# A new engine order, fewer filling matmuls and fewer normalisation shifts in a recurrent attention and gated MLP kernel

## Chip, core and metric

The kernel runs on one core of a Trainium2 chip. The metric is device time in microseconds (us), median over runs. The names of the engines are PE (TensorE), DVE (VectorE), ACT (ScalarE), POOL (GpSimd) and SP (SyncE, which here only issues DMAs).

## What is computed

A gated linear recurrence over 768 steps for 4 batches and 8 heads of width 48, followed by a gMLP block whose spatial mixing runs over the 768 steps:

```python
for t in range(S):                      # B, H, S, D = 4, 8, 768, 48
    state = alpha[:, :, t, :, None] * state + einsum('bhd,bhe->bhde', k[:, :, t], v[:, :, t])
    y[:, :, t] = einsum('bhd,bhde->bhe', q[:, :, t], state)
x = y.transpose(0, 2, 1, 3).reshape(B, S, H * D)
h = maximum(x @ w_in, 0.0)              # 384 -> 1024
u, v = h[..., :512], h[..., 512:]
v_n = (v - mean(v)) / sqrt(var(v) + 1e-06)
v_s = einsum('ts,bsd->btd', w_spatial, v_n) + b_spatial[None, :, None]
out = ((u * v_s) @ w_out)               # 512 -> 384, float32
```

## The kernel before

The recurrence is worked in chunks of 128 steps, six to a batch, 24 in all. Inside a chunk the decays are summed as logarithms by a matmul with a triangle (`cum`, and `half` for the first part of a sum over two), and the exponentials of the sums scale the keys (`kt` = k times the inverse product `binv`) and the queries (`qt`). Matmuls then make transposes of both (`tr`, `trk`), the chunk's contribution to the state (`upd`), masked scores (`sc`; the mask is applied by DVE: `ms`, `m`) and the output (`y`), which also takes the state before it. The state goes on in DVE and POOL: `z` adds the old state, `S` multiplies by the chunk's decay, `sb` copies it to bf16. Chunks 0 to 3 and 6 to 9 are worked four at a time (`four_chunks`), chunks 4 and 5 as a pair, the others two by two; a `j` in a key counts pairs of chunks, an `i` single chunks. The first number of a key in the MLP is the batch.

The MLP has for each batch the projections `v` (with its eviction `ve`) and `u` (`ue`), normalisation (`bn` statistics on DVE, `rs` the reciprocal deviation on ACT, `nm` the shift, `vn` the normalised rows), spatial mixing `s(b, d, th, part)` (the product with the transposed spatial weights: four matmuls, then two), its eviction with bias `se` on DVE, the gate `g` (tile gT) on POOL or DVE, and the output projection `o` with eviction `oe` and store. The weights come in float32 and are cast (`cast`); the spatial weights are transposed by PE (`wt`) and evicted (`we`).

Nothing here is scheduled by the framework. All operations are collected in a list `ops`, and the string `PLAN` gives the order in which they are emitted: a word is an engine's letter (P, D, A, G for POOL, S for SP) and the operation's number, after `@` the PSUM banks that it takes, after `:` filling matmuls ahead of it, written as columns, kind and bank (`512#7`: a float32 matmul of 512 columns on constant data into bank 7). Each engine works its own instructions in the order in which the words stand. Most evictions and products may run on one of two or three engines, and the letter decides which. `replay` reads the plan. Helpers record all matmuls of the projections and of the mixing on line 1006, all PSUM copies on lines 179 and 181, the products with `mul` on line 190, the filling matmuls on line 243, the shifts on line 1085, `vn` on lines 1093 (ACT) and 1097 (DVE).

`vn` has two forms. On ACT it is scale times input plus a shift, and needs the shift −mean/deviation; on DVE it subtracts the mean and multiplies, and does not read the shift:

```python
                if e == "ACT":
                    nc.scalar.activation(
                        out=vn[n2][:, x, :], in_=v_sb[n2][:, x, :], func=AF.Identity, bias=shift[n2][:, x:x + 1],
                        scale=rstd[n2][:, x:x + 1])
                    return
                nc.vector.tensor_scalar(
                    out=vn[n2][:, x, :], in0=v_sb[n2][:, x, :], scalar1=mvs[n2][:, x, 0:1],
                    scalar2=rstd[n2][:, x:x + 1], op0=ALU.subtract, op1=ALU.mult)
```

Of the kernel before, what the change touches and what calls it, by code (L numbers as in the profile page):

```python
# [37 lines left out]
LETTERS = {"P": "PE", "D": "DVE", "A": "ACT", "G": "POOL", "S": "SP"}  # L38
# [1 line left out]


PLAN = """
D2 D0 D4 D1 G9 G11 G5 G6 D3 S56 S57 S59 S58 A60 S12 S169 S170 A61 S272 S171 D8 P62@0:512#0:512#0:512#0 P66@1 P67 P63
P70@2 P71 P74@3 P75 A68 A64 D79 G82 P91@4,5 P52@6 A69 A72 A76 G7 A78 A92 A84 A65 G88 G87 A73 A77 D85 D90 D81 D93 D53
D83 D80 P103@6,4,5,7:512#7:424#7 P94@0,1 D86 D104 D89 D106 G13 P97@6,2:192#2 D98 A95 P100@3,0 D101 A96 P117@3,6:376#1
P115@4,1 A99 G107 G14 A15 A173 D102 D109 P128@0,2 D119 D118 P174@5 A116 A122 A176 P130@6,4 S16 D132 D131 S172 A135
P175@1 A129 P120@3 P54@2 G110 G105 P136@0,4 A121 A178 A55 G111 G108 P133@6 G181 A180 A134 G184 A179 D112 A177 D138
P123@7,3 P141@2 S20 G276 G277 G278 G17 G19 G18 D124 D125 P151@6 P187@7,4 P126@3 S23 S274 S273 D185 A152 A127 G186 G183
G113 G114 D182 P190@5,6 A189 A192 A142 P144@3 D137 P139@4 D188 D191 A140 G22 G21 D153 D143 P199@6,5 P196@2,7 P162@4
A280 A145 P287@0 A163 P154@1 P160@3 A279 A288 A155 D200 D201 D198 D197 D164 P193@4 A161 P156@7 A157 A165 D194 D146  # L50
P158@5 A159 G195 P202@1,2 P203 S26 A204 A147 D166 P290@4 P37@5,7 D38 P34@3,6 G24 S275 S384 S396 G25 S503 S29 D35
P207@1 D148 D208 D36 A39 A289 P205 P281@7 P40@3,5 A206 A282 A167 G10 D42 P210@2 D149 D150 D41 S385 S386 D168 D209 S398
S397 P284@5 P223@6 P219@3 P221@1 A211 A291 A224 A285 D212 A283 A220 A213 D295 D301 A286 A292 D214 D222 D215 A216
P225@6 P233@2 P217@3 P229@7 P237@0 A218 A28 D298 G297 G27 D304 G294 P226 D227 G300 G303 P43@3,5 D45 P230 P234 D231
D235 A293 A44 P46@4,6 P306@5,1 D308 P238 P49@7,3 D50 D51 A48 A47 A307 P309@2,6 P315@1,4 P312@5,7 P249@3 P250 A310 A316
A314 A296 A311 A299 D313 D317 D239 G236 D251 P338@4,1 P332@7,5 P245@0 P246 G302 G305 D333 D339 G232 P318@7,6,3,2 G240
G228 D340 D319 A507 G33 D334 D321 D247 P253@4 P330@7,1 P254 P241@5 P242 G320 A388 A400 A30 A337 A331 A32 G322 P389@0
D255 P345@7,6 D243 D324 D347 A390 P341@4 A391 P335@5 G31 G325 D394 D327 D346 G393 P401@3 A342 A336 A402 A403 P257@1
A392 S492 S387 A258 P259@4 P356@2 S399 G404 G248 G323 G326 S491 S557 P343@0,7 D405 P351@3,5 P407@1,6 A357 D328 A344
A350 A408 D353 D352 P359@2 G252 G395 P348@7 A349 P354@3 D409 S505 S494 S506 P418@6,1 P413@5,0 D358 S493 S504 S559 S547  # L60
S545 S608 S558 S548 S546 A355 A360 D415 D420 P508@7 P366@3 P410@0 P371@2 P377@1 D411 D414 A260 A509 P375@0 D419 A495
D361 A372 A561 P262@5 P496@6 G244 G329 G406 G256 A367 A376 A510 D368 G412 A497 A498 P416@0 P421@3 A422 G514 G502 G500
D378 D379 D513 G512 A417 P264@2 P267@4 A499 A362 A380 A268 D363 D501 P426@0 P423@1 P435@3 P437@6 D381 A365 A427 A424
P433@4 A434 A438 A382 D263 D436 P269@0 D364 D265 D425 D428 D383 P518@1 P369@4 A511 A270 P562@6 P373@2 A374 A429 A549
P439@7 A565 P526@0 D440 D519 P453@3 D430 D431 A432 A563 A564 D370 P449@7 P550@1 P515@2,5 A516 A551 A553 D517 A552 P454
D455 D527 D567 G566 G520 G554 G456 P441@4 P442 P445@5 D443 P450 D451 P465@6 P446 D555 D447 P530@7,4 P521@2,0 P569@1,3
D522 G448 G452 P469@5 P466 P457@2 P470 D523 D531 D532 G528 G444 D471 S620 A556 P572@7 D573 A570 P458 S622 S609 S560
A612 D467 D459 P613@4 P524@5 P533@1 A624 S610 A571 P576@7,3 P585@6,0 G574 A614 A525 D586 A615 A534 P625@5 A626 A568
G472 P535@2 A627 P461@1 S621 S611 S727 S715 S718 S623 S717 G617 D618 D578 D577 S730 S729 P473@6 G628 G575 P538@3
P581@7 A536 A616 A539 P462 S781 S716 A474 D629 P631@5,4 D587 A633 D463 D582 S728 A719 P588@3 S783 S769 S782 S770 S832  # L70
S771 A589 S784 S772 G619 G529 P579@1 A580 D632 D537 P634@7 P479@6 A630 A480 P720@5 G583 G468 D635 G636 A721 P642@3,4
P637@0,2 D540 G460 G584 P476@7 P601@6 P593@1 D643 D639 D638 A731 A723 D644 G726 G464 A602 A738 G724 P590@3 P597@6 A591
P732@0 D603 D592 A735 D477 P645@4 P640@3 A541 D542 D543 D594 A646 P485@2 A641 A785 A598 A486 D544 P650@4 P657@7 P742@6
A651 D743 D652 A733 A604 D605 D607 P488@3 P661@4 A658 A662 A734 P647@6 A489 A773 G736 P595@1 D648 D606 P482@4 D649
A483 A722 D744 P663@7 A664 D737 P599@6 P659@4 P786@3 A653 A600 P673@7 P669@0 P750@6 A596 A787 A788 P774@1 A775 A789
A776 S481 S844 S833 S834 A836 A780 S835 S845 A660 S846 D654 D655 D656 D751 D725 P674 P670 P677@6 P685@5 D671 P678
P665@0 D791 D752 D675 D779 G778 G792 D679 P796@7 P666 G790 D797 P686 G672 D687 D667 P739@6,4 P793@7,3 A848 A777 D794
P693@5 A740 A795 G680 G676 P805@0 P694 P849@7 P837@6 A838 A839 A850 A840 A851 D741 P745@3,4 P754@1,2 D695 G798 G668
D746 D806 D755 P689@5 P690 D691 D747 P681@3 P700@0 P682 P697@5 G843 D756 A698 D683 P703@4 D853 D842 D704 A701 P757@5
A758 P748@0 A749 A799 P800@6,7 D802 G841 G852 P809@3,2 P855@4,5 G807 G684 G696 G688 A856 G692 D810 P759@0 S847 P858@7  # L80
P762@3 D811 D801 P709@2 P812@6 A753 A760 P803@0 A857 D859 D761 D854 A813 A804 A763 P861@5,7 P866@4,1 S699 P712@6 D863
# [51 lines left out]
def kernel(  # L133
# [23 lines left out]
    NDS = DH // 128  # L157
# [70 lines left out]
    vn = sb("vn", 2, [128, NT, DH])  # L228
# [37 lines left out]
    ops, made = [], {}  # L266
# [788 lines left out]
    def project_v(b, tt):  # L1055
# [20 lines left out]
        def rs(_):  # L1076
# [3 lines left out]

        op(("rs", b, tt - 1), "ACT", rs,
           [("bn", b, tt - 1), ("bn", b, tt), ("vn", b - 2, tt - 1), ("vn", b - 2, tt), ("zeros", 3)])
        def nm(_):
            for x in (tt - 1, tt):
                nc.vector.tensor_scalar(
                    out=shift[n2][:, x:x + 1], in0=mvs[n2][:, x, 0:1], scalar1=rstd[n2][:, x:x + 1], scalar2=-1.0,
                    op0=ALU.mult, op1=ALU.mult)
# [188 lines left out]
```

## Time and profile before

| | us |
|---|---|
| median of 3 runs | 138.48 |
| lowest, highest | 137.95, 138.50 |
| profiled execution | 139.19 |
| its span in the trace | 137.4 |
| PE, DVE, ACT, POOL busy | 131.0, 120.8, 108.0, 87.2 |

The span is the time from the first to the last instruction in the trace; what the profiled execution took beyond it lies around it. Lines of the profile name the source line, the engine, the operation, and the tiles as out<-in without buffer numbers. In a timeline the first number is the start, the second the time that the row's instructions cover; a bracket at the end gives idle time ahead of the row and what ended it. In a table of groups stand count, busy time, mean duration in ns, and idle time ahead. The ends of matmuls are modelled, so the distance between starts says more than a matmul's own length.

### The profile page before, as it was taken

To read this page: it belongs to the slowest core of one execution; us is meant where nothing else is said; L and a number is where in the kernel's file an instruction comes from. 1 tells how busy PE (TensorE), PEld (TensorE's weight loads), DVE (VectorE), ACT (ScalarE), POOL (GpSimd) and SP (SyncE) were. 2 spreads that over 40 slices of the span, in tenths; PEclk is the share of its full clock that TensorE was granted. 3 is DMA by queue.
4 is the path that set the end of the run, shared out by engine and by line. 5 is a ranking of instruction groups with operands and counts; after the bars stand their busy time and mean duration, and the time that the engine had idled before them with its cause. 6 is when DMAs were issued, how large, how long until landed. Compare 5 with 4: busy or idle time off the path is not lost.

```text
span 137.4 us, 5308 instructions
## 1 busy us (share of the span) xinstructions
PE 131.0 (95%) x2122; PEld 79.2 (58%) x2122; DVE 120.8 (88%) x300; ACT 108.0 (79%) x261; POOL 87.2 (63%) x146
## 2 busy tenths in 40 slices
PE   6899998999999999999999999999999999999990
PEld 3365554564646566566657666656566765565560
DVE  6259999979999999999899999997999999974871
ACT  3476998899989889999997989999965796954041
POOL 7365899967399789972079989620799842003560
PEclk9999999999999999999999999999999999999999
DMA  3999999599989796899999797899991497101055
GB/s 83 371 371 382 341 321 347 132 374 383 366 164 261 159 218 127 163 184 192 195 190 209 143 205 147 167 194 226 190 181 23 158 390 257 66 0 57 0 203 203
DMA packets 76473, 28.66 MB, mean 209 GB/s; under 512 B 63008, under 2 KB 74912, under 8 KB 76448
## 3 DMA queue, kind: packets, MB, share of 16 engines
q1 hardware_dynamic: 76416, 28.32, 78.6%
q8 instruction: 16, 0.26, 0.8%
q14 instruction: 9, 0.07, 0.2%
q0 software_dynamic: 32, 0.00, 0.0%
HBM read 23.60 MB, written 4.72 MB: 206 GB/s over the span
## 4 chain that ended last, share of the span: by engine, by line
PE 76%; ACT 6%; DVE 6%; DMA 5%; issue 3%; POOL 2%; SPq 0%; POOLq 0%; ACTq 0%
PE bank L1006 53%; DMA kc<-in_k_dram 5%; PE bank L961 3%; PE bank L945 3%; PE bank L989 3%; PE bank L417 2%; PE bank L855 2%; PE bank L899 2%; PE bank L837 2%; PE bank L933 2%; DVE vn L1097 1%; PE bank L795 1%; PE bank L772 1%; ACT uT L185 1%; DVE w_spT L181 1%
## 5 line engine op out<-in xcount | busy, mean ns | idle before, releaser
L1006 PE MATMUL bank<-w_spT,vn 128*128 128x384 bf16 x192 | 35.8, 327 | 0.3 <-DVE vn L1097 0.3
L190 POOL TENSOR_TENSOR gT<-vs,uT 128x384 bf16<-128x384 f32 x28 | 25.7, 933 | 14.3 <-DVE vs L1153 14.1
L190 POOL TENSOR_TENSOR kt<-kc,binv 128x384 bf16<-128x384 f32 x22 | 20.3, 931 | 20.3 <-ACT binv L909 15.2
L1006 PEld LDWEIGHTS <-vn 128*128 128x128 bf16 x192 | 17.4, 98 | 11.7 <-DVE vn L1097 0.7
L1006 PE MATMUL bank<-w_in,xT 128*128 128x512 bf16 x72 | 19.1, 380 | 0.2 <-ACT xT L179 0.2
L1006 PE MATMUL bank<-xT,w_in 128*128 128x384 bf16 x96 | 18.7, 326 | 0.0
L1006 PE MATMUL bank<-w_out_sb,gT 128*128 128x384 bf16 (+1 forms) x100 | 18.4, 320 | 0.0
L1153 DVE TENSOR_TENSOR vs<-bank,bsp_bc 128x384 f32<-128x384 f32 x31 | 16.3, 550 | 2.4 <-PE bank L1006 2.3
L950 DVE TENSOR_TENSOR ptm<-bank,mask 128x512 bf16<-128x512 f32 x28 | 17.9, 683 | 0.4 <-PE bank L945 0.2
L179 ACT COPY kqT<-bank 128x512 bf16<-128x512 bf16 (+1 forms) x20 | 15.0, 792 | 3.1 <-PE bank L989 1.9
L1068 DVE BATCH_NORM_STATS2 stats<-v_sb 128x6 f32<-128x512 bf16 x24 | 16.4, 682 | 0.2
L185 ACT ACTIVATE v_sb<-bank 128x512 bf16<-128x512 f32 x20 | 11.8, 599 | 1.8 <-PE bank L1006 1.5
L185 ACT ACTIVATE uT<-bank 128x384 bf16<-128x384 f32 x27 | 12.4, 495 | 0.7 <-PE bank L1006 0.6
L1006 PEld LDWEIGHTS <-w_in 128*128 128x128 bf16 x96 | 9.0, 98 | 6.7 <-DVE ptm L950 0.3
L190 DVE TENSOR_TENSOR qt<-qc,bank 128x384 bf16<-128x384 f32 x24 | 12.6, 545 | 0.2 <-DMA qc<-in_q_dram 0.2
L1006 PEld LDWEIGHTS <-gT 128*128 128x128 bf16 x100 | 9.3, 98 | 5.8
L179 ACT CAST xT<-bank 128x384 bf16<-128x384 f32 x23 | 10.4, 482 | 1.8 <-PE bank L417 1.4
L844 DVE TENSOR_TENSOR ptm<-bank,mask 128x512 bf16<-128x512 f32 x16 | 10.4, 684 | 0.0
L1006 PEld LDWEIGHTS <-xT 128*128 128x128 bf16 x72 | 6.2, 97 | 6.2 <-ACT xT L179 1.2
L179 ACT COPY raw_w<-bank 128x384 f32<-128x384 f32 x8 | 3.8, 480 | 7.3 <-PE bank L1006 7.2
L394 DVE TENSOR_TENSOR zs<-bank,state 128x384 f32<-128x384 f32 x16 | 8.8, 549 | 0.5 <-PE bank L933 0.4
L243 PE MATMUL bank<-junk 128*128 128x512 f32 (+3 forms) x14 | 8.0, 700 | 1.1 <-DVE junk L1242 1.1
(162 smaller groups left out, 265.4 us busy)
## 6 DMA issues: line engine op xcount, KB each, us to landing
ac<-in_alpha_dram SPq DMA_DIRECT2D x14, 192.0 KB, 4.4
kc<-in_k_dram SPq DMA_DIRECT2D x14, 192.0 KB, 4.0
qc<-in_q_dram SPq DMA_DIRECT2D x14, 192.0 KB, 4.4
vc<-in_v_dram SPq DMA_DIRECT2D x14, 192.0 KB, 4.1
raw_w<-in_moe_w_spatial_dram SPq DMA_DIRECT2D x3, 768.0 KB, 8.0
out_dram<-o_sb SPq DMA_DIRECT2D x9, 192.0 KB, 2.0
ac<-in_alpha_dram SPq DMA_DIRECT2D x2, 768.0 KB, 6.8
kc<-in_k_dram SPq DMA_DIRECT2D x2, 768.0 KB, 7.6
```

The costliest lines, as they stand in the source:

```text
L179: nc.scalar.copy(out=out, in_=in_)
L185: nc.scalar.activation(out=out, in_=in_, func=AF.Relu)
L190: ENG[eng].tensor_tensor(out=out, in0=in0, in1=in1, op=ALU.mult)
L243: nc.tensor.matmul(out=banks[n][:, 0:cols].rearrange("p (a b) -> p a b", a=4), lhsT=junk, rhs=junk[:, None, 0:cols // 4].to_broadcast([128 ...
L394: lambda _: nc.vector.tensor_tensor(out=zs[i % 3], in0=tp(), in1=state[(i - 1) % 3], op=ALU.add),
L844: nc.vector.tensor_tensor(out=ptm[n2][:, ci, s], in0=banks[sl.bank].rearrange("p (hp t) -> p hp t", hp=HP), in1=mask[:, 3][:, None, :].to_ ...
L945: nc.tensor.matmul(out=pt[s][:, hp, :], lhsT=kT[rows, hp, :], rhs=qT[rows, hp, :], start=True, stop=True)
L950: nc.vector.tensor_tensor(out=ptm[n2][:, ci, s], in0=banks[sl_p[s].bank].rearrange("p (hp t) -> p hp t", hp=HP), in1=mask[:, 2][:, None, : ...
L961: nc.tensor.matmul(out=place(to, 3 * hp + (0, 1, 1, 2)[x]), lhsT=heads(vb, hp, x), rhs=ptm[n2][:, ci, x // 2, hp, :], start=(turn == 0), s ...
L1006: nc.tensor.matmul(out=ps, lhsT=lhsT, rhs=rhs, start=first and n == 0, stop=last and n == len(pairs) - 1)
L1068: nc.vector.bn_stats(out=stats[tt % 2], in_=v_sb[n2][:, tt, :])
L1153: nc.vector.tensor_tensor(out=vs[d], in0=banks[sl.bank][:, 0:TH], in1=bsp_bc[:, th, :], op=ALU.add)
```

## The change

Three things are changed.

- `PLAN` is a new string. The order on SP is the same as before; on PE, DVE, ACT and POOL it is another, and so are banks. For a number of operations the engine is another. Over the whole run DVE gets five more key products (`kt`, `kts`: 2 before, 7 after) and four more gates (4, then 8) from POOL, four more `vn` from ACT (18, then 22), and gives three `ve` to ACT (4, then 1) and two `S` to POOL; POOL gives five of its 13 `sb` to ACT or DVE. POOL has 111 operations before and 97 after, ACT 234 and 237.
- The filling matmuls stand at the same places. Ahead of the first sums they have 512, 512 and 512 columns before and 512, 512 and 360 after; ahead of the first state update 512 and 424, then 512 and 160; ahead of the transposes of the second keys 192, then 104; ahead of the first scores 376, then 232.
- The shift `nm` was one operation for two row tiles and always computed both (24 instructions). It is now one operation for each row tile and emits nothing where the `vn` of that tile runs on DVE. `vn` runs on ACT for two tiles after, so two shifts are left. `replay` sets each operation's engine ahead of the replay so that `nm` can see it.

```diff
 PLAN = """
-D2 D0 D4 D1 G9 G11 G5 G6 D3 S56 S57 S59 S58 A60 S12 S169 S170 A61 S272 S171 D8 P62@0:512#0:512#0:512#0 P66@1 P67 P63
-P70@2 P71 P74@3 P75 A68 A64 D79 G82 P91@4,5 P52@6 A69 A72 A76 G7 A78 A92 A84 A65 G88 G87 A73 A77 D85 D90 D81 D93 D53
...
+S56 D0 S57 G6 D1 S59 G10 D2 D3 G5 S58 G9 D8 D4 A60 G11 S12 A61 P62@0:512#0:512#0:360#0 P70@1 P66@2 P63 P67 A64 P71
+S171 A68 P74@3 D79 A72 P75 D82 S172 D85 P91@4,5 A76 P52@6 G87 A93 D88 G90 A53 D92 A84 D81 G7 S275 A77
...
 """
...
 def replay(ops, held, warm, plan):
 
+    for word in plan.split():
+        op = ops[int(re.match("[A-Z]([0-9]+)", word).group(1))]
+        op.eng = LETTERS[word[0]]
     for word in plan.split():
...
-        def nm(_):
-            for x in (tt - 1, tt):
+        for x in (tt - 1, tt):
+            def nm(_, x=x):
+                if made[("vn", b, x)].eng == "DVE":
+                    return
                 nc.vector.tensor_scalar(
                     out=shift[n2][:, x:x + 1], in0=mvs[n2][:, x, 0:1], scalar1=rstd[n2][:, x:x + 1], scalar2=-1.0,
                     op0=ALU.mult, op1=ALU.mult)
 
-        op(("nm", b, tt - 1), "DVE", nm, [("rs", b, tt - 1), ("vn", b - 2, tt - 1), ("vn", b - 2, tt)])
-        for x in (tt - 1, tt):
+            op(("nm", b, x), "DVE", nm, [("rs", b, tt - 1), ("vn", b - 2, x)])
+
             def vnf(e, x=x):
...
             op(("vn", b, x), "DVE ACT", vnf,
-               [("rs", b, tt - 1), ("nm", b, tt - 1)] + [("s", b - 2, d, th, 1) for d in range(NDS) for th in range(2)])
+               [("rs", b, tt - 1), ("nm", b, x)] + [("s", b - 2, d, th, 1) for d in range(NDS) for th in range(2)])
```

More of the change, by code (lines that the diff above doesn't have):

```diff
@@ L48 @@
[L48 to L57, printed above, removed]
@@ new lines @@
+D187 P139@1 A145 D184 G19 A17 D18 G281 P192@4,2 D191 S23 P157@5 A194 D193 S277 A140 D146 P201@2,4 G185 A282 S276
+P198@7,6 P161@1 G188 D202 A153 G114 P159@0 D200 A283 G22 P195@2 D203 P163@6 A162 D196 A147 P155@1 A160 G197 D150 D199
+P287@2 A158 D154 P204@7,0 A164 G21 A288 P207 D165 P205 G24 P37@6,5 A208 S26 P34@4,3 A206 D151 D148 S278 P212@0 G25
+A289 D38 S389 D39 A166 P209@7 A213 D169 D35 D36 P224@4 D167 D149 A210 S401 D214 P293@0 A156 P290@3 A225 P43@7,5 D301
+A168 P40@1,6 P222@4 D45 D170 A41 P226@5 D211 A291 P284@1 A42 P220@2 G303 A294 P236@6 A215 A285 D216 D218 D227 D44 D306
@@ new lines @@
+A374 D386 A446 S555 D518 P524@4 P272@0 A429 D380 A376 P569@3 D367 S553 P431@2 A520 D388 A268 D430 P459@5 A432 P451@1
+A572 D433 S628 A570 P467@2 A571 A434 P455@7 S630 A556 D437 D507 D525 D438 D435 P532@6 P447@4 A273 S617 D436 D533
+P557@0 D573 P452 G534 S567 A558 P441@6 D574 A620 P448 D453 A563 P460 S618 G561 D449 A560 P521@3,1 A559 D461 P468 G454
+S629 A632 D562 P579@5 A442 P456 D580 G450 A523 P463@0 S619 D469 P633@5 D522 P439@6 G462 S736 A634 P464 D457 A440
+P527@3,1 D465 P576@2,4 S724 G458 D529 P536@6,7 A577 P475@0 G526 D537 S727 G581 P621@1 D538 A575 P443@6 S631 A635 D578
@@ new lines @@
+P476 A622 P471@7 D528 A623 G625 P472 A627 D637 P588@3 P485@4 A444 D477 G636 A624 D626 P530@6 S726 A486 P539@0 G466
+D473 A531 P592@4,1 D589 A728 S739 P639@7,5 G474 D594 A540 P583@3,6 A740 P541@2 D593 S738 G478 A641 P642@1 D640 P741@4
+S791 P544@0 G590 A542 D584 A535 P479@7 D470 G591 S725 A742 D585 P482@3 A545 G582 D643 P729@2 S737 G638 A483 P595@0
+D546 A480 G735 P586@3 S793 A596 D543 P650@7,1 A730 P645@0,6 A587 P608@5 D652 A547 P600@3 A743 D647 S779 A732 P494@1
+D651 G733 A795 P597@6 S792 D646 A495 G644 A731 P491@7 D746 A744 S780 D734 D548 D550 G745 P796@0 A598 P602@4 A609 S843
@@ new lines @@
+P648@6 G747 A601 D610 P653@5 P748@3,2 A654 D599 P751@1 A492 S781 P658@5 A603 D752 A649 P604@7 A659 S794 P759@6 P666@1
+A611 A749 P655@5 S782 D614 D612 D753 D549 D750 D660 P670@2 A656 D615 S487 P606@3 D613 A797 D551 P488@5 A667 D657 G800
+S855 A783 P672@4 S844 A798 D671 P678@1 A607 S845 A661 P784@2 P682@3 A847 D664 D801 D662 D489 D665 A785 P674@5 S846
+D663 A787 G788 D760 A786 P683 S856 A799 P675 D789 G761 P686@6 A605 D684 A673 P679 S857 D676 A790 G685 P754@4,3
+P803@7,2 D755 S858 G677 P763@5,0 A804 P687 D680 P668@4 D688 A802 P690@1 D765 G689 A859 P691 D764 P848@0 G681 P694@6
@@ new lines @@
+P718@2 A836 D775 D778 P885@0 D837 A719 P895@7 A838 P882@2 D839 D841 D886 D840 P715@0 A883 D842 P897@3 A776 D884 P893@2
+A830 P909@5 D887 A898 A896 P921@6 D894 A832 A888 P901@7 A722 D889 D891 D892 P905@4 A716 D890 S723 P913@0 S717 P910
+P914 D911 P902 P906 D915 G912 P899@5 D903 P917@0 D907 A900 G904 D916 P918 P922 P929@5 D919 P930 D908 G920 P925@0 D923
+P926 D931 P938@6 D927 P932@5 D928 A939 D924 P935@0 S940 A933 P941@6 S934 D936 S720 P947@5 A942 S937 P944@0 D948 S943
+P950@5 A945 S949 A951 S946 S952
```

54 lines of the change are left out of this document (20 added, 34 removed).

## The prediction

> **What bounds the kernel now.** I read the page first, then busy time by stage, then the order of time on single engines.
>
> ```profile
> span 137.4 us, 5308 instructions
> PE 131.0 (95%) x2122; PEld 79.2 (58%) x2122; DVE 120.8 (88%) x300; ACT 108.0 (79%) x261; POOL 87.2 (63%) x146
> PE 76%; ACT 6%; DVE 6%; DMA 5%; issue 3%; POOL 2%; SPq 0%; POOLq 0%; ACTq 0%
> ```
>
> The chain that ended last is three quarters TensorE (PE), but VectorE (DVE) is busy 88%. By stage (engine busy us in each stretch):
>
> ```profile
> core 0: us, PE busy (x) PEld busy (x) DVE busy (x) ACT busy (x) POOL busy (x), PEclk, DMA share, GB/s
> 8.40:15.40 7.00, 6.76 (x158) 4.06 (x155) 6.79 (x15) 5.55 (x14) 4.90 (x9) 1.00 1.11 366
> 15.40:25.00 9.60, 8.66 (x228) 5.02 (x231) 9.36 (x19) 8.33 (x21) 9.32 (x15) 1.00 1.02 327
> 25.00:38.50 13.50, 13.20 (x212) 7.30 (x202) 12.48 (x34) 13.20 (x33) 9.16 (x17) 1.00 0.97 313
> 38.50:60.00 21.50, 21.46 (x501) 13.46 (x502) 21.00 (x44) 19.74 (x47) 19.05 (x27) 1.00 0.85 179
> 8.40:96.30 87.90, 86.38 (x1604) 52.86 (x1602) 84.11 (x192) 80.49 (x200) 63.22 (x91) 1.00 0.95 235
> 96.30:134.20 37.90, 37.83 (x506) 23.25 (x504) 33.21 (x72) 23.63 (x57) 19.92 (x38) 1.00 0.47 140
> ```
>
> From 38.5 us PE has no gap worth naming. Up to 96.30 DVE is free for only 87.90 − 84.11 = 3.79 us, of which 0.21 + 0.24 + 1.02 fall before 38.5 and 2.32 after, where it mostly waits for a later PE. So two engines are nearly full over 88 us, and PE is the one that sets the end. I therefore cut the run at one block that both versions have: s(2,2,0,1), the second part of batch 2's first mixing product, which needs the last normalised rows vn of batch 2 from DVE.
>
> ```profile
> 8.40 1.55 DVE L190 TENSOR_TENSOR kt<-kc,binv 128x384 bf16<-128x384 f32 x2 [3.59 <-ACT binv L741]
> 95.16 0.73 DVE L1097 TENSOR_SCALAR vn<-v_sb,mvs,rstd 128x512 bf16<-128x512 bf16 x2
> 96.32 1.14 PE L1006 MATMUL bank<-w_spT,vn 128*128 128x384 bf16 x6
> 134.22 0.36 DVE L181 COPY raw_w<-bank 128x192 f32<-128x192 f32 x1 [0.62 <-PE bank L1006]
> ```
>
> DVE starts its stream at 8.40 and has those vn at 95.89; PE begins the block at 96.32 and is done at 134.22, where the last eviction starts: 37.9 us. What follows (eviction, store) is the same in both versions.
>
> **The part before the block, on PE.** Fillers first:
>
> ```profile
> 10.05 1.84 PE L243 MATMUL bank<-junk 128*128 128x512 f32 x4
> 11.82 0.26 PE L795 MATMUL bank<-o_sb,kt 32*128 32x96 bf16 x8
> 12.33 0.78 PE L795 MATMUL bank<-o_sb,kt 32*128 32x96 bf16 x56 [0.24 <-POOL o_sb L181]
> 13.38 0.59 PE L243 MATMUL bank<-junk 128*128 128x192 f32 x2
> 14.61 0.90 PE L243 MATMUL bank<-junk 128*128 128x376 f32 x2
> 15.44 0.40 PE L837 MATMUL bank<-kqT 48*128 48x128 bf16 x8
> ```
>
> After 10 us they go from 512+424+192+376 = 1504 columns to 512+160+104+232 = 1008. 936 columns occupy 10.05 to 11.82, 1.9 ns a column, so 496 columns are 0.9 us. But they stand where PE would wait: the state update after the first pair waits again at 12.33 for GpSimd's (POOL) cast of v, and the scores at 15.44 need evictions of the same queue of DVE and ACT work. In the new order all four kt of the first quad run on DVE and both casts of v's second half on POOL.
>
> ```profile
> 9.50 0.49 ACT L741 ACTIVATE binv<-bank 128x384 bf16<-128x384 f32 x1 [0.34 <-PE bank L701]
> ```
>
> The last of the four exponentials that kt needs is done at 10.0. I walk DVE from there, at 0.36 to 0.6 us an operation: the fourth kt to 10.7, an eviction and a cast to 11.4 (the state update can start), two qt, the first state and two qt to 14.1, a sum to 14.6, two evictions to 15.25. So the scores start at 15.3: a gain of 0.1 us (0 to 0.9), with the fillers hidden in both versions.
>
> Second, a change of tile shape on PE. Non-filling blocks change shape 81 times before and 72 after:
>
> ```profile
> 80.09 0.49 PE L1006 MATMUL bank<-w_spT,vn 128*128 128x384 bf16 x2
> 80.51 0.41 PE L989 MATMUL bank<-ident,kt 64*128 64x64 bf16 x16
> 102.24 0.49 PE L1006 MATMUL bank<-w_spT,vn 128*128 128x384 bf16 x2
> 102.56 0.49 PE L899 MATMUL bank<-la,le_one 128*128 128x384 bf16 x2
> ```
>
> The same two matmuls hold PE 0.42 us before another shape and 0.32 before their own: 0.1 each, 0.9 for nine, some of it given back where two small blocks that had run into each other are parted. Seven of the nine lie before s(2,2,0,1). From the scores to the block PE took 96.32 − 15.44 = 80.9 us, 1.3 of it idle by the stage rows; less that and the 0.7, and with 0.7 of work that now stands ahead of the block (below), it could be there at 15.3 + 80.9 − 1.3 − 0.7 + 0.7 = 94.9. It counts only if DVE is there too.
>
> **The part before the block, on DVE.** I count DVE operations from the first kt to the last vn of batch 2 in both orders. Rows for the prices (min/median/max where three numbers stand):
>
> ```profile
> L1085 DVE TENSOR_SCALAR shift<-mvs,rstd 128x1 f32<-128x1 f32 x24 | 3.9, 206 | 1.0 <-ACT rstd L1079 1.0
> L1097 DVE TENSOR_SCALAR vn<-v_sb,mvs,rstd 128x512 bf16<-128x512 bf16 x18 | 7.6, 443 | 0.0
> L187 DVE TENSOR_SCALAR v_sb<-bank 128x512 bf16<-128x512 f32 x4 | 2.7, 673 | 0.0
> L181 DVE COPY kqT<-bank 128x1024 bf16<-128x1024 bf16 x5 | 3.3, 683 | 0.2 <-PE bank L989 0.2
> L190 DVE TENSOR_TENSOR qt<-qc,bank 128x384 bf16<-128x384 f32 x24 | 12.6, 545 | 0.2 <-DMA qc<-in_q_dram 0.2
> ```
>
> ```profile
> L190 DVE TENSOR_TENSOR kt<-kc,binv x2: 636/816/995, 8.4 to 9.3; 128x384 bf16<-128x384 f32 x2
> L190 DVE TENSOR_TENSOR gT<-vs,uT x3: 549/550/1096, 128.1 to 130.6; 128x384 bf16<-128x384 f32 x3
> ```
>
> Neighbours on DVE overlap by 0.08 us (0.995 + 0.636 stand in 1.55), which I take off each price. Gone: 17 of 18 shifts, 17 × 0.126 = 2.1; three v_sb evictions to ACT, 3 × 0.59 = 1.8. New: four vn from ACT, 4 × 0.36 = 1.45; five key products from POOL, three near the short price 0.56 and the median 0.74, two at 0.74: 3.35 (2.8 to 4.6); two gT at 0.47, 0.95 (to 2.0). Two 128x1024 evictions (0.60) and two qt (0.47) now stand ahead of the block, 2.1 in all. Five small operations leave and six come, each between an eviction of 0.3 and a qt of 0.5; I set them against each other. Net +3.95 (3.4 to 5.9). POOL loses some 14 operations, so fewer collide with DVE; for that I take 0.2 off: +3.75.
>
> DVE's first kt is released by the first of two exponentials in either order, at 8.35. Idle: the 2.32 us after 38.5 go, since DVE is now the later one; of the 1.47 before I keep 0.6 (0 to 3.8 in all). Part of it is one load:
>
> ```profile
> 35.70 0.91 POOL L190 TENSOR_TENSOR kt<-kc,binv 128x384 bf16<-128x384 f32 x1 [1.53 <-DMA kc<-in_k_dram]
> ```
>
> The order of SyncE's loads is unchanged, so these keys land at 35.7 again. One product of them now stands on DVE, at about 34.7 to 35.7 by the count of what precedes it, and behind it queue the last two vn of batch 0 and four qt, on which the mixing of batch 0 and the transposes wait: 0 to 1.0.
>
> **The sum.** DVE has the last vn at 8.35 + 84.1 + 3.75 + 0.6 = 96.8, later than the 94.9 of PE, so PE waits for it and starts s(2,2,0,1) at 96.85 against 96.32. From there PE has less to do: the transposes of chunks 18 and 19 (0.5) and one four-matmul product (0.65) are already done, one three-matmul block (0.49) is not, and two changes of shape go: 37.9 − 0.7 − 0.2 = 37.0. The last eviction starts at 133.85 against 134.22: 0.4 us less. The profiled execution took 139.19 (span 137.4), so it would take 138.8; the median of the runs, 138.48, becomes **138.1**. PE's savings are real, but most of them turn into waiting for DVE. ±0.5% is 0.7 us, about what a measurement of this kernel can tell from no change: the forecast is no change with a slight lean to faster; its own range is 137.5 to 138.9.
>
> **The rivals.** *Faster: DVE loses nothing.* If the new order leaves DVE neither idle nor colliding, the terms are 8.35 + 84.1 + 3.4 − 1.2 (of what collisions cost in the 84.1; the vn just ahead of 38.5 and one kt alone lost 0.6 and 0.35) = 94.65, and PE's own 94.9 ends last: 131.9, 2.3 less, 136.2; halfway to the forecast, 137.1. For it: POOL, the partner in collisions, gets 10 us lighter; against it: no stage before 60 us shows DVE without idle.
>
> *Slower: the moved products collide.*
>
> ```profile
> 129.29 1.97 POOL L190 TENSOR_TENSOR gT<-vs,uT 128x384 bf16<-128x384 f32 x2 [1.68 <-DVE vs L1153]
> ...
> 130.58 1.10 DVE L190 TENSOR_TENSOR gT<-vs,uT 128x384 bf16<-128x384 f32 x1
> ```
>
> A gT on DVE beside one on POOL took 1.10 us where it takes 0.55 alone. The change moves such products from POOL to DVE, among POOL's others. If five of the seven ahead of the block pay 0.5 each, that is 2.5, of which 0.55 stands in the prices above (three at 0.74 instead of 0.56); the block starts 1.95 later: 140.0. It decides from 0.4 us of such loss on; at 1.1 the kernel is slower by over 0.5%.
> The Trainium skill, "SBUF — State Buffer", section "Who interferes with whom", says that a DVE instruction with two SBUF inputs contends with a GpSimd instruction that reads SBUF. By that rule all seven would be exposed whenever POOL works (63.22 of 87.90 us), which is this rival's case; the row above agrees with it.
>
> *Slower: PE goes cold.* The first fillers ran at up to 1.2 us where the median is 0.6:
>
> ```profile
> L243 PE MATMUL bank<-junk x14: 326/592/1222, 1.1 to 15.0; 128*128 128x512 f32 x8, 128*128 128x424 f32 x2, 128*128 128x192 f32 x2, 128*128 128x376 f32 x2
> ```
>
> With a third fewer filling columns PE could fall back to that pace between 10 and 16 us; 3.4 us of work at half pace is 1.7 us later: 139.8. Against it: the holes left are 0.2 to 0.5 us each, and the clock stood at 1.00 in all stretches.
> The Trainium skill, "TensorE: Matmul & The Clock Gate", section "What's actually happening", has the clock halved after an idle window of about 3.4 us; by that rule holes this short do not do it.
>
> *It does nothing:* fewer fillers and changes of shape only lengthen PE's waits, and DVE ends where it did: 138.5, inside the forecast's range.
>
> **How the numbers follow.** Forecast and "nothing" 0.42, DVE without loss 0.32, colliding products 0.23, cold PE 0.03. The range 136.6 to 140.0 takes most of the faster case and the slower one to four fifths. Faster by over 0.5%: the 0.32 and a little of the forecast's low end, 0.36; within: 0.37; slower: 0.27.
>
> **What would show it.** Right: DVE busy over 97% from 15 to 95 us, PE with small waits on DVE (vn, ptm, kqT) throughout, the first scores at 15.3, s(2,2,0,1) near 96.9, then 37 us to the end. Wrong: PE without gaps and this block before 95.5 (DVE lost less than I charge), or kt and gT on DVE near 1.0 us and the block after 97.5, or a clock under 1.00 after 5 us.

## The result and the profile after

The changed kernel is slower: 139.5 us median of 20 runs (138.66 to 141.37) against 138.34 of 20 for the kernel before (137.85 to 139.71), run beside each other; ratio 1.0075, 95% interval [1.0047, 1.0103]. Runs in which TensorE's clock was cut (two of the 20, at 0.972) or which lie over 1.5% above their kernel's fastest are left out of the ratios and of the pooled counts below. The forecast was 138.1, no change with a lean to faster.

And yet the profiled execution of the changed kernel took 138.68 us, 0.5 less than the 139.19 of before's, and 0.1 from the 138.8 that the sum gave. Its page:

```profile
span 136.9 us, 5254 instructions
PE 129.4 (95%) x2108; PEld 79.2 (58%) x2122; DVE 119.8 (88%) x289; ACT 108.3 (79%) x264; POOL 77.8 (57%) x132
PE 80%; DVE 7%; ACT 6%; DMA 3%; issue 1%; ACTq 0%
```

The same stretches as before, engine busy us in each (14 matmul records are missing here, so PE's figures are a little low):

```profile
core 0: us, PE busy (x) PEld busy (x) DVE busy (x) ACT busy (x) POOL busy (x), PEclk, DMA share, GB/s
8.40:15.40 7.00, 6.18 (x160) 4.25 (x158) 6.05 (x14) 6.27 (x17) 3.16 (x7) 1.00 1.11 365
15.40:25.00 9.60, 8.80 (x205) 4.87 (x205) 9.51 (x20) 9.26 (x22) 8.85 (x12) 1.00 1.02 335
25.00:38.50 13.50, 13.22 (x237) 8.07 (x238) 13.29 (x35) 13.38 (x34) 8.16 (x12) 1.00 1.01 319
38.50:60.00 21.50, 21.34 (x490) 13.68 (x492) 21.10 (x47) 19.12 (x49) 17.04 (x25) 1.00 0.96 198
8.40:96.30 87.90, 85.43 (x1629) 53.46 (x1639) 84.67 (x189) 81.58 (x208) 55.92 (x77) 1.00 0.98 240
96.30:134.20 37.90, 36.80 (x466) 22.56 (x468) 31.94 (x66) 23.61 (x54) 17.41 (x35) 1.00 0.41 131
```

GpSimd lost 7 us up to 96.30, VectorE gained only 0.56, and ScalarE now stands at 81.58, three microseconds below VectorE. The checkpoints, from the timeline (start, duration, engine):

```profile
8.71 0.56 DVE L194 TENSOR_TENSOR kt<-kc,binv 128x384 bf16<-128x384 f32 x1 [3.94 <-ACT binv L745]
15.73 0.49 PE L841 MATMUL bank<-kqT 48*128 48x128 bf16 x5
95.49 0.73 DVE L1103 TENSOR_SCALAR vn<-v_sb,mvs,rstd 128x512 bf16<-128x512 bf16 x2
95.30 1.96 PE L1010 MATMUL bank<-w_spT,vn 128*128 128x384 bf16 x11
133.11 0.70 ACT L183 COPY raw_w<-bank 128x384 f32<-128x384 f32 x2 [0.50 <-PE bank L1010]
```

VectorE has the last vn of batch 2 at 96.22. TensorE's row at 95.30 has six matmuls of 0.163 us ahead of s(2,2,0,1), which so starts at 96.27, without a gap. The last eviction ends at 133.81; before it ended at 134.58. The prices held: no kt on VectorE collided, and one gT of seven did (min/median/max):

```profile
L194 DVE TENSOR_TENSOR kt<-kc,binv x7: 547/552/590, 8.7 to 67.4; 128x384 bf16<-128x384 f32 x7
L194 DVE TENSOR_TENSOR gT<-vs,uT x7: 543/551/1035, 44.4 to 130.6; 128x384 bf16<-128x384 f32 x7
```

So the two profiles say "0.5 us faster" and the runs say "1.0 us slower". Before's profile (139.19) lies 0.85 above the median of the 20 runs (138.34), after's (138.68) 0.82 below its own (139.5). The experiments had to find where the time is lost when like is compared with like, and whether VectorE holds TensorE up, as the forecast had it.

### The profile page after: what moved, and what is told of

The parts are those of the page before. It is cut to its first block, busy times and chain, and to the rows that moved or that the text cites. A ratio compares the mean times of both kernels' runs of the same rounds, so it can differ in the third digit from the quotient of the medians.

```text
span 136.9 us, 5254 instructions
## 1 busy us (share of the span) xinstructions
PE 129.4 (95%) x2108; PEld 79.2 (58%) x2122; DVE 119.8 (88%) x289; ACT 108.3 (79%) x264; POOL 77.8 (57%) x132
## 4 chain that ended last, share of the span: by engine, by line
PE 80%; DVE 7%; ACT 6%; DMA 3%; issue 1%; ACTq 0%
PE bank L1010 54%; DMA ac<-in_alpha_dram 3%; PE bank L949 3%; DVE qt L194 2%; PE bank L722 2%; PE bank L993 2%; PE bank L965 2%; PE bank L421 2%; DVE ptm L848 2%; PE bank L841 2%; PE bank L903 2%; PE bank L937 1%; PE bank L859 1%; ACT kqT L183 1%; PE bank L819 1%
## 5 line engine op out<-in xcount | busy, mean ns | idle before, releaser
L194 POOL TENSOR_TENSOR gT<-vs,uT 128x384 bf16<-128x384 f32 x24 | 21.8, 925 | 14.2 <-DVE vs L1159 14.0
L194 POOL TENSOR_TENSOR kt<-kc,binv 128x384 bf16<-128x384 f32 x17 | 15.6, 930 | 15.3 <-ACT binv L913 10.9
L1010 PE MATMUL bank<-xT,w_in 128*128 128x384 bf16 x96 | 19.7, 326 | 0.0
L1010 PE MATMUL bank<-w_in,xT 128*128 128x512 bf16 x58 | 17.1, 380 | 1.5 <-issue 0.5
L189 ACT ACTIVATE v_sb<-bank 128x512 bf16<-128x512 f32 x23 | 13.5, 601 | 0.9 <-PE bank L1010 0.9
L848 DVE TENSOR_TENSOR ptm<-bank,mask 128x512 bf16<-128x512 f32 x16 | 10.2, 677 | 0.0
L194 POOL TENSOR_TENSOR state<-zs,bc 128x384 f32<-128x384 f32 x6 | 5.3, 875 | 8.3 <-DVE zs L398 8.3
L183 ACT COPY raw_w<-bank 128x384 f32<-128x384 f32 (+1 forms) x11 | 5.0, 470 | 5.3 <-PE bank L1010 5.3
```

What stands on the lines that cost most here:

```text
L183: nc.scalar.copy(out=out, in_=in_)
L189: nc.scalar.activation(out=out, in_=in_, func=AF.Relu)
L194: ENG[eng].tensor_tensor(out=out, in0=in0, in1=in1, op=ALU.mult)
L848: nc.vector.tensor_tensor(out=ptm[n2][:, ci, s], in0=banks[sl.bank].rearrange("p (hp t) -> p hp t", hp=HP), in1=mask[:, 3][:, None, :].to_ ...
L1010: nc.tensor.matmul(out=ps, lhsT=lhsT, rhs=rhs, start=first and n == 0, stop=last and n == len(pairs) - 1)
```

## Experiments: the edits that stand by themselves

**e1, nothing changed.** The changed kernel once more, for a second profile.

> The changed kernel once more, unaltered, for a second trace beside its times. Theory A (the new order leaves DVE no cushion, so whatever differs from one execution to the next, a landing or a collision, reaches the end): times spread over 138.7 to 140.5, and a trace whose execution is slower than the first one's 138.7 loses its time in PE waiting for DVE or ACT at several places between 15 and 100 us. Theory B (with fewer filling columns PE's clock is sometimes late or falls back): the slower trace shows a granted clock below 1.00 or matmuls at half pace before 16 us, and afterwards runs like the first trace. Theory C (a load lands later and everything follows): the slower trace is shifted from the landing on by one step.

Measured: ratio 1.0068 [1.0041, 1.0096], profile 138.63 us. The theories speak of an execution slower than 138.7, and this one is not, so none of them is decided here; the profiles of e2, e5 and e12 serve for that below.

**e2 and e3, the fillers.**

```diff
# e2: the changed kernel with the old fillers
-P62@0:512#0:512#0:360#0   P103@4,6,5,7:512#7:160#7   P97@4,2:104#4   P117@0,3:232#6
+P62@0:512#0:512#0:512#0   P103@4,6,5,7:512#7:424#7   P97@4,2:192#4   P117@0,3:376#6
# e3: the kernel before with the new fillers, the reverse
```

> The changed kernel with the filling matmuls of the kernel before (512, 512, 512; 512, 424; 192; 376 columns) at its own places and in its own banks. Theory B (cold clock): 138.0 to 138.6, ratio to before about 1.00, less spread, clock 1.00 in all executions. Theory A (no cushion on DVE): 139.5 to 140.0 as the changed kernel, since DVE sets the pace; up to 0.5 more if the longer fillers stick out.

> The kernel before with the filling matmuls of the changed one (512, 512, 360; 512, 160; 104; 232 columns). Theory B (cold clock): slower by 0.5 to 1.2 us, with clocks of 0.97 to 0.998 in some executions. Theory A: 138.0 to 138.4, no change, since the fillers stand in PE's waits.

Measured: e2 1.0079 [1.0052, 1.0106]; e3 1.0017 [0.9987, 1.0047]. The fillers make no difference that can be measured in either kernel; theory B, a cold clock, falls for e2. e3's profile (137.86 us, clock 1.0) is the least disturbed one of the old order, and below it stands for it.

**e4, the shifts.** The kernel before, with a shift only where ScalarE normalises (18 fewer).

```diff
             for x in (tt - 1, tt):
+                if made[("vn", b, x)].eng == "DVE":
+                    continue
```

> The kernel before with the shift computed only for the six row tiles whose vn runs on ACT: 18 shifts fewer on DVE, 18 x 0.126 = 2.3 us of DVE time, the order unchanged. If DVE and PE bound the kernel jointly before (the reading of the prediction), 0.3 to 1.0 us faster, most of it before 40 us; if PE alone does, 138.3, no change.

Measured: 1.0041 [1.0010, 1.0073]. In the old order, 18 instructions less on VectorE are not a gain.

**e5, the last eviction.**

```diff
-P950@5 A945 S949 A951 S946 S952
+P950@5 A945 S949 D951 S946 S952
```

> The changed kernel with one letter different: the very last eviction, oe(23,1), runs on VectorE as in the kernel before, and not on ScalarE. From the start of TensorE's last block to the end of the span the changed kernel's two profiles show 3.97 and 3.93 us, the kernel before 3.72 and 3.74. Theory (part of the loss is this tail): the stretch falls to about 3.75 us, the time by about 0.2 us against the changed kernel (ratio to the kernel before 1.0055 or less, where the unchanged changed kernel showed 1.0068). Rival (the last store's landing sets the tail, whoever evicts): the stretch stays at 3.9 to 4.0 and the ratio at 1.007.

Measured: 1.0061 [1.0024, 1.0098], and the stretch from TensorE's last block (133.58) to the end of the span (137.51) is 3.93 us. The engine of the last eviction is not the cause of the longer tail. Of the rival, the stretch is as expected, the ratio lies between the two.

**e12, the product that waits for its keys.** kt(4,1) behind the last two vn of batch 0 on VectorE.

```diff
-... D216 D218 D227 D44 D306 P228@7 D217 A292 S509 D219 P232@5 ...
+... D216 D218 D227 D44 P228@7 D217 A292 S509 D219 D306 P232@5 ...
```

> The changed kernel with one operation moved on VectorE: kt(4,1), which waits for the keys that land at about 35.7 to 36.8, runs behind the last two vn of batch 0 instead of ahead of them. The prediction gave that wait 0 to 1.0 us; in the profile of the changed kernel with the old fillers it was 0.56, and the two vn behind it took 1.32 instead of 0.73. Theory D (the changed kernel is slow mainly in the executions in which these keys land late): median 0.3 to 0.6 us lower, the spread between runs smaller, ratio to the kernel before 1.002 to 1.005. Rival (the keys' landing shifts all that follows, wherever the product stands): ratio 1.006 to 1.008, spread as before.

Measured: 1.0084 [1.0055, 1.0112]. No gain; the rival holds. Why, the timelines show. First e1 (undisturbed), VectorE and GpSimd:

```profile
35.54 0.56 DVE L194 TENSOR_TENSOR kt<-kc,binv 128x384 bf16<-128x384 f32 x1
36.02 0.73 DVE L1103 TENSOR_SCALAR vn<-v_sb,mvs,rstd 128x512 bf16<-128x512 bf16 x2
34.77 0.91 POOL L194 TENSOR_TENSOR kt<-kc,binv 128x384 bf16<-128x384 f32 x1 [3.38 <-ACT binv L745]
```

Then e2, where the keys landed later:

```profile
36.28 0.56 DVE L194 TENSOR_TENSOR kt<-kc,binv 128x384 bf16<-128x384 f32 x1 [0.56 <-DMA kc<-in_k_dram]
36.75 1.32 DVE L1103 TENSOR_SCALAR vn<-v_sb,mvs,rstd 128x512 bf16<-128x512 bf16 x2
36.29 1.31 POOL L194 TENSOR_TENSOR kt<-kc,binv 128x384 bf16<-128x384 f32 x1 [4.72 <-DMA kc<-in_k_dram]
37.81 1.96 PE L1010 MATMUL bank<-w_spT,vn 128*128 128x384 bf16 x10 [0.35 <-DVE vn L1103]
```

One landing releases a key product on both engines, and the vn behind it take 1.32 us beside GpSimd instead of 0.73; TensorE waits. And e12, VectorE and GpSimd:

```profile
35.95 1.02 DVE L1103 TENSOR_SCALAR vn<-v_sb,mvs,rstd 128x512 bf16<-128x512 bf16 x2
36.88 0.55 DVE L194 TENSOR_TENSOR kt<-kc,binv 128x384 bf16<-128x384 f32 x1
35.58 0.91 POOL L194 TENSOR_TENSOR kt<-kc,binv 128x384 bf16<-128x384 f32 x1 [4.25 <-DMA kc<-in_k_dram]
```

VectorE's wait for the keys is gone, but the vn still meet GpSimd's product: 1.02. The Trainium skill, "SBUF — State Buffer", section "Who interferes with whom", counts tensor_scalar among the VectorE operations that can enter a mode which takes the port pair shared with GpSimd; vn is one, and these rows agree. The forecast had looked at the two-input products alone.

## Experiments: which engine sets the pace

**e6, all 24 shifts again in the new order.** The two added lines that skip the shift are taken out.

```diff
-                if made[("vn", b, x)].eng == "DVE":
-                    return
```

> The changed kernel with all 24 normalisation shifts issued again, so that VectorE has some 2.7 us more work, nearly all of it ahead of s(2,2,0,1). Theory A (the prediction's: VectorE sets the pace from 8.4 us to s(2,2,0,1), TensorE waits for it): s(2,2,0,1) comes 1 to 2.5 us later than the 96.1 to 96.3 of the changed kernel's two profiles and the ratio to the kernel before rises to 1.014 to 1.02. Theory B (TensorE never waits from 43 us on; its own stream of blocks sets the time, and VectorE's 96% is work that has room between its due times): s(2,2,0,1) moves by 0.4 us at most and the ratio stays within 1.005 to 1.010.

Measured: 148.87 us, ratio 1.0745 [1.0717, 1.0773], far beyond either. Busy time and idle time before it, then VectorE's waits between 8.4 and 106 us:

```profile
L1089 DVE TENSOR_SCALAR shift<-mvs,rstd 128x1 f32<-128x1 f32 x24 | 4.5, 208 | 6.2 <-ACT rstd L1083 6.2
DVE shift L1089 <- ACT rstd L1083: 5.2, 8, 1.7
```

The new order puts the shift's word right behind ScalarE's rstd, which costs nothing while the word emits nothing. Emitted, it adds 4.1 us of work (22 × 0.19) and 6.2 us of waiting, and 10.2 us arrive at the end (148.95 against 138.7 of the profiles). What is added here finds no room; the run does not separate the work from the waiting that its place in the order brings.

**e8, work taken from VectorE.** Six products back on GpSimd.

```diff
-... D306 ... D243 ... D518 ... D573 ... D470 ... D697 ...
+... G306 ... G243 ... G518 ... G573 ... G470 ... G697 ...
```

> The changed kernel with six of the products that it moved to VectorE back on GpSimd, at the same places of the order: kt(4,1), kts 13 and 15, and the gates g(0,3,0), g(1,1,1), g(2,1,1). VectorE loses some 3.3 us of work. Theory A (VectorE sets the pace): 0.5 to 1.5 us faster than the changed kernel, ratio to the kernel before 0.996 to 1.003. Theory B (TensorE's stream sets the time): s(2,2,0,1) within 0.4 us of the changed kernel's, ratio 1.005 to 1.009.

Measured: 1.0077 [1.0048, 1.0106]: no change against the changed kernel. Theory A, VectorE sets the pace, falls. In its profile the same VectorE operations start only 0.2 us earlier against e1 at 128 us than at 44 us (the granted clock was 1.00 in that stretch), for 3.3 us of work taken off.

**e7, work added to TensorE.** Ten filling matmuls of 128x256.

```diff
-P428@7       P451@1       P447@4       P541@2       P608@5
+P428@7:256=7 P451@1:256=1 P447@4:256=4 P541@2:256=2 P608@5:256=5
```

> The changed kernel with ten more filling matmuls (128x256 bf16, full array, two each ahead of v(1,4), s(1,1,0,0), s(1,0,0,0), v(2,0) and v(2,3), between 61 and 84 us), the work of no other engine changed. They take TensorE 1.0 to 1.3 us (128x384 takes 0.163 us from one to the next, so 128x256 some 0.11). Theory B (TensorE's stream sets the time): the whole of it arrives at the end, ratio to the kernel before 1.014 to 1.017. Theory A (VectorE sets the pace): under 0.3 us arrives, ratio 1.007 to 1.009.

Measured: 1.0134 [1.0088, 1.0179], 0.9 us above the changed kernel's 1.0068 (0.0066 × 138.45): most of the 1.1 arrives, a little below what theory B expected; the interval also reaches A's. The profile, one of the slower executions, shows more: the ten fillers hold TensorE 1.1 us (0.11 from one to the next), yet the lag behind e1 grows from 0.9 us at 44 us to 2.8 at 96.

**e9, e10, e11, work taken from TensorE.**

```diff
-                accumulate(flat(sl)[:, 0:w], [
-                    (gT[b % 2][:, d, tt * 128:(tt + 1) * 128], w_out_sb[:, d, cols]) for d in range(NDS)])
+                for d in range(NDS):
+                    n = 128 if b < 2 and d in (1, 2) else w
+                    nc.tensor.matmul(out=flat(sl)[:, 0:n], lhsT=gT[b % 2][:, d, tt * 128:(tt + 1) * 128],
+                        rhs=w_out_sb[:, d, cols.start:cols.start + n], start=d == 0, stop=d == NDS - 1)
```

> The changed kernel with less work on TensorE alone: in the 12 output products o of batches 0 and 1 (47 to 91 us) the second and third matmul take 128 columns instead of 384, so part of the output is left uncomputed; every weight load, wait, eviction and store stays. 24 matmuls, each shorter by about 0.10 us (384 columns follow one another at 0.163 us; loads of 128 columns at about 0.06): some 2.3 us. Theory B (TensorE's stream alone sets the time, VectorE's work has room): the time falls by 2.0 to 2.4 us against the changed kernel, ratio to the kernel before 0.989 to 0.993. Theory C (both engines are full to the same us, so that taking work from either one alone brings little): it falls by under 1 us, ratio above 1.000.

> The same shortening of 24 matmuls (part of the output left uncomputed), and the six products back on GpSimd, so that TensorE and VectorE are both relieved, by some 2.3 and 3.3 us. Theory B: no more than with TensorE relieved alone, within 0.4 us of it. Theory C: the time falls by 1 us or more beyond it, to a ratio of 0.989 to 0.993.

> The kernel before with the same shortening of 24 matmuls (part of the output left uncomputed). It has 3.8 us in which VectorE is free up to s(2,2,0,1). Theory B: it falls by the same 2.0 to 2.4 us as the changed kernel does (ratio 0.983 to 0.986). Theory C in the form that the change used up VectorE's room: it falls by clearly more than the changed kernel does, by 0.7 us or more. If VectorE was as near in the kernel before, it falls by under 1 us as well (ratio above 0.993).

Measured: e9 1.0057 [1.0019, 1.0094]; e10 1.0072 [1.0045, 1.0099]; e11 0.9988 [0.9957, 1.0019]. That TensorE was relieved is plain: the 48 output matmuls between 44 and 97 us in e1 and in e10, then e10's page:

```profile
L1010 PE MATMUL bank<-w_out_sb,gT 128*128 128x384 bf16 x48 | 9.5, 326 | 0.0
```

```profile
L1185 PE MATMUL bank<-w_out_sb,gT 128*128 128x384 bf16 (+1 forms) x48 | 6.9, 273 | 0.0
PE 127.2 (93%) x2108; PEld 78.4 (57%) x2122; DVE 118.5 (87%) x283; ACT 108.2 (79%) x264; POOL 82.3 (60%) x138
PE 55%; ACT 17%; DVE 9%; DMA 6%; POOL 5%; issue 3%; SPq 2%; ACTq 0%; POOLq 0%; DVEq 0%
```

2.6 us less work on TensorE, and s(2,2,0,1) comes at 96.15 in e10, as in e1 (96.07). The chain that ended last has 55% TensorE where e1 had 81%: ScalarE, VectorE and GpSimd step in. Between 44 and 128 us the profiles gain 0.1 us on e1 in e9 (granted clock 1.00 there) and 0.4 in e10, and 0.4 on e3 in e11; e10 lay 0.4 behind at 44 us, which is why its block comes no earlier. Theory B, TensorE's stream alone sets the time, falls too, and so does C as it was put (relief on both brings 0.4 us and not 1).

**e17 and e18, ScalarE.** Seven evictions of u (A374, A446, A376, A601, A603, A667, A607) become D374 and so on, on top of e10 and of e8.

> As e10 (six products back on GpSimd, 24 output matmuls shortened so that part of the output is left uncomputed), and seven evictions of u, at 62 and at 88 to 94 us, on VectorE instead of ScalarE: ScalarE loses about 3 us, VectorE has as much work as in the changed kernel. Theory C3 (three engines full to the same microsecond, ScalarE the third): 0.8 us or more below e10, ratio to the kernel before 1.001 or less. Rival (whatever is relieved, the fixed order of the queues takes it back): ratio 1.005 or more.

> As e17 with the output matmuls whole, so the whole result is computed: ScalarE relieved by 3 us, VectorE as full as in the changed kernel, TensorE as in it. Theory C3: TensorE is full, so it stays within 0.4 us of the changed kernel (ratio 1.004 to 1.010) and e17 lies 0.8 us or more below it. Rival: e17 and this one are equal within 0.4 us.

Measured: e17 1.0256 [1.0213, 1.0299]; e18 1.0293 [1.0251, 1.0335]. The two lie 0.5 us apart, with intervals that overlap, much as the rival expects, but both went up by some 2.5 to 3 us: seven evictions of 0.54 on VectorE at those places cost two thirds to four fifths of their 3.8 us, although VectorE had been relieved of 3.3 elsewhere. So whether ScalarE alone would be the next bound is not shown; that VectorE has no room at the very places where it is given more is shown once more.

## Experiments: which stretch loses it

**e13 to e16**, one order up to a block, the other behind it, words that are already done left out, a bank renamed where it is still held:

```diff
# e13: words of the new plan up to s(0,1,0,0), then the old plan's remaining words; e14 the reverse
# e15: words of the new plan up to s(2,2,0,1), then the old plan's remaining words; e16 the reverse
```

> The new order (and its fillers) up to the mixing product s(0,1,0,0), at 36 us, the old order from there on; five PSUM banks are renamed where the two are joined, and shifts go only to the rows that ScalarE normalises (as in the kernel before with fewer shifts, ratio 1.004). Theory S (the start holds the loss: more spread in the stretch in which the loads saturate): ratio 1.007 to 1.009. Theory M (the loss is in the middle, where TensorE now has eight small waits): 1.000 to 1.004. Theory E (the loss is behind 96 us): 1.000 to 1.004.

> The old order (and its fillers) up to s(0,1,0,0), the new order from there on; seven banks renamed at the joint. Theory S: 1.000 to 1.004. Theory M: 1.006 to 1.009. Theory E: 1.006 to 1.009.

> The new order up to s(2,2,0,1), at 96 us, the old order behind it; two banks renamed at the joint. Theories S and M: 1.006 to 1.009. Theory E: 1.000 to 1.004.

> The old order up to s(2,2,0,1), the new order behind it; three banks renamed at the joint. From the profiles, the stretch behind the block shows 0.2 us more between TensorE's last block and the end of the span in the new order, and nothing else: ratio 1.000 to 1.004 by theories S and M. Theory E: 1.006 to 1.009.

Measured: 1.0194 [1.0158, 1.0230], 1.0233 [1.0199, 1.0268], 1.0202 [1.0163, 1.0241], 1.0278 [1.0215, 1.0340]. All four are 2 to 3% slower, so their totals answer nothing. Waits just behind the joint hold the loss; what PE waited for in e13 (two of its rows) and in e16 (one):

```profile
PE bank L1029 <- DVE vs L1166: 1.7, 1, 1.7
PE bank L848 <- DVE vs L1166: 0.3, 1, 0.3
```

```profile
PE bank L1000 <- ACT uT L196: 2.7, 1, 2.7
```

Six to ten operations out of step at one place cost 2 us and more that are never made good.

The undisturbed profiles do tell. Starts in us, read from the traces (the last block by its row less the matmuls ahead of it):

```
                                   scores   last block of PE   end of span   time
e3, old order                       15.23             132.36        136.08   137.86
e1, new order                       15.52             132.71        136.64   138.63
new less old, from point to point   +0.29              +0.06         +0.21    +0.21
```

From the scores to the last block the new order takes 117.2 (after, e1), 118.0 (e5, e12) and 118.3 (e2), the old one 117.1 (e3), 118.0 (e4) and 118.2 (before). So over 117 us of work an undisturbed execution neither gains nor loses by the change. The start is not worse either, and e3's is an early one: in the profiles of all runs the scores come at 15.39 to 15.79 where the start is the new order's (14 profiles, median 15.54), and at 15.23 to 15.87 where it is the old one's (6, median 15.57).

The disturbed profiles of the new order lose their time between 18 and 40 us, and the loss goes with the landing of the queries and keys that the prediction followed to 35.7 us. Issue and time to landing of the keys in e1, then in e2:

```profile
25.67 0.58 SPq L675 DMA_DIRECT2D kc<-in_k_dram  x1
kc<-in_k_dram SPq DMA_DIRECT2D x1, 768.0 KB, 8.8
```

```profile
26.62 0.58 SPq L675 DMA_DIRECT2D kc<-in_k_dram  x1
kc<-in_k_dram SPq DMA_DIRECT2D x1, 768.0 KB, 9.5
```

Five profiles, with a granted clock of 0.995 or more, have the new order unchanged up to 60 us. Where the keys land at 33.8 (after) and 34.5 (e1), nothing is lost; where they land at 35.5 (e7), 35.7 (e5) and 36.2 (e2), 1.0, 0.7 and 1.2 us are. The queries land at 31.1 and 31.4 in the first two, at 32.5 to 33.4 in the others. In the old order e3 and e11 lose nothing with keys that land at 35.0 and 35.2, while before and e4 lose over a microsecond, a part of it ahead of 32 us. So the new order seems to need these loads earlier. That is read from a few profiles and not shown by an experiment: e12 moved only one of the products that wait for them, and its profile lost 0.8 us with keys landing at 35.4.

## Why the prediction was wrong, by its own steps

**The step that failed is the last one of the sum:** "The profiled execution took 139.19 … so it would take 138.8; the median of the runs, 138.48, becomes 138.1". An execution of this kernel can lose about a microsecond between 16 and 48 us (behind that, the profiles of one order keep step to 0.1 us), and before's profile is one that did: 1.1 us longer from the scores to the last block than e3. The new order was measured against that, and the difference was carried over to the medians as if the runs of both orders were disturbed alike, which they are not (below, under Open). The 138.8 was met (138.68, 138.63), but by luck, as one of the best executions of the new order, in which the keys landed early; its like in the old order is e3's 137.86. Like against like, from e3 to e1, the sum's −0.14 at the scores, −0.23 up to the last eviction and nothing behind it stand against +0.29 (chance, see above), +0.06 and +0.42.

**TensorE alone, 94.9: too early by 1.4.** It came to 96.27 without a gap ahead of it. 0.43 of that is the scores, at 15.73 and not 15.3. Another part is the 1.3 us of idle that the step struck out: the stage rows of after still leave 0.80, 0.28 and 0.16 free (a little less, for the missing records). The seven changes of shape, worth 0.7, are not seen either: between 46 and 131 us, counting for each change what the step to the next matmul takes beyond the median step of that form without a change (waits that fall there included), the 39 to 41 changes in three profiles of the old order (before, e3, e4) cost 4.8 to 5.2 us, and the 35 to 37 in three of the new one (after, e1, e2) 4.7 to 5.2. Fewer changes, each a little dearer.

**VectorE, 96.8: too late by 0.6.** It had the last vn at 96.22. That is close by luck: two errors of opposite sign are in it. From its first kt to that vn it worked 84.58 us, 0.5 more than before (84.11) and not 3.75, but it stood idle for 2.9 us where the sum kept 0.6. Of the work, and with 0.08 taken off for each as in the prediction, the five more key products came to 1.9 and not 3.35 (0.55 each, none collided), the four more vn to 0.6 and not 1.45 (before's vn hold the one of 1.01 shown below), and the small operations, set against each other, to −0.4. So VectorE did not become the later engine that TensorE waits for; the two arrive within 0.05 us of one another.

**"It counts only if DVE is there too" was half of it.** The sum took the later of two engines as the end. e8 to e11 show that neither is: 2.6 us less work on TensorE, 3.3 less on VectorE, or both, bring 0.1 to 0.4 us in the changed kernel's profiles and at most 0.25 in its ratios (e9's interval reaches 0.7), and 0.2 to 0.35 in the kernel before (e11, by ratio and by medians; its interval includes no change), while more work arrives nearly whole or more than whole (e6, e7). This fits queues in a fixed order that wait for each other in turn, so that the time is that of a chain through all of them, as e10's chain shows; which operation holds which was not isolated.

**"What follows is the same in both versions" was wrong by 0.2 in the span:** from the end of the last eviction to the end of the span 2.84 (before, e3), but 3.04 (after, e1), 3.05 in e5. The last two stores show where. First e3, whose last eviction ends at 133.24, then e1, where it ends at 133.60:

```profile
133.06 0.35 SPq L1195 DMA_DIRECT2D out_dram<-raw_w  x1
133.50 0.38 SPq L1195 DMA_DIRECT2D out_dram<-raw_w  x1
```

```profile
133.53 0.41 SPq L1201 DMA_DIRECT2D out_dram<-raw_w  x1
134.03 0.41 SPq L1201 DMA_DIRECT2D out_dram<-raw_w  x1
```

In e1 SP's queue begins the store ahead only 0.07 us before the last eviction ends (0.18 in e3) and takes longer over it, so the last store follows the last eviction by 0.43 us and not 0.26; from there to the end of the span both take 2.6. e5 shows 0.44, so it isn't the last eviction's engine. And outside the span lie 1.79 us on the mean in the kernel before, 1.94 (the 20 runs) and 2.00 (e1) in the changed one; the cause of that was not found.

**Right:** the fillers are hidden (e2, e3); the products that were moved don't collide as the slower rival had it (kt 0.55); the clock stood at 1.00 in the profile; "it does nothing" holds for fillers (e2, e3), shifts (e4) and, by the steps above, changes of shape, each. The rival "slower" had the right partner in the wrong place: it is the two vn beside GpSimd's key product that lose 0.3 (e12) to 0.6 (e2), and the old order has a like collision, with GpSimd's cast of a weight row. Before's timeline:

```profile
37.47 1.01 DVE L1097 TENSOR_SCALAR vn<-v_sb,mvs,rstd 128x512 bf16<-128x512 bf16 x1
37.51 0.82 POOL L181 CAST w_row<-raw_w 128x768 bf16<-128x768 f32 x1 [0.90 <-DMA raw_w<-in_moe_w_spatial_dram]
```

And e3's, where the vn is done before the cast starts:

```profile
36.60 0.41 DVE L1097 TENSOR_SCALAR vn<-v_sb,mvs,rstd 128x512 bf16<-128x512 bf16 x1
36.93 0.82 POOL L181 CAST w_row<-raw_w 128x768 bf16<-128x768 f32 x1 [0.87 <-DMA raw_w<-in_moe_w_spatial_dram]
```

**Open.** In the runs that are counted the mean is 138.35 us (121 runs of the kernel before) and 139.39 (25 of the changed one), 1.04 more. An undisturbed execution can be estimated from the rows above: the median start, the stretch of e3 or e1 to the last block, the tail and what lies outside give 15.57 + 117.13 + 3.72 + 1.79 = 138.2 for the old order and 15.54 + 117.20 + 3.93 + 1.95 = 138.6 for the new one. So 0.4 of the 1.04 is not disturbance, and nearly all of that lies behind TensorE's last block. The other 0.6 would be disturbance: the mean lies 0.1 above the estimate in the old order and 0.8 in the new one, and 59 of 121 runs lie within 0.5 us of the fastest before, 7 of 25 after. The late landings above are the likely cause of it; which operations of the new order make it sensitive was not isolated.

## What to carry to other kernels

Before a difference between two profiles is carried to a median, place each profile among its own runs: here they lay 0.85 above and 0.82 below, together more than the effect. In this kernel, where VectorE, ScalarE and TensorE are busy over 90% up to 96 us, 2.6 us off one engine brought 0.1 to 0.4, while additions were paid in the main (two thirds of their work in e17, more than their work in e6); count a change by what it adds where its queue is full, not by its net sum. Neither of these two orders could be joined to the other without losing 2 to 3%.

## What was not expected of the hardware and the order

An instruction of 0.2 us cost twice its duration when its place in the order was ahead of its input: 22 more shifts, 4.1 us of work and 6.2 us of waiting, 10 us in the end (e6). Two vn that take 0.73 us together took 1.02 beside one GpSimd product of the usual 0.91 (e12), and 1.32 beside one that itself took 1.31, where a key product on VectorE had started with it (e2). And 2.6 us less matmul work, on the engine that holds 81% of e1's chain, did not move the end (e10).
